# Turning two row groups of the first batch by DMA transposes, and loading batch 2's rows in quarters, in a spectral-filter and feed-forward kernel

## The chip, the cores and the metric

One Trainium2 chip, one of its cores. The metric is the device time of one launch in microseconds (us), the median of several runs. Runs of one kernel on one core agree to within some 0.3% here; the kernel before gave 776.29 to 777.75 us in the first three.

## The reference

For each of 8 batches of 3008 rows of 256 numbers, a real Fourier transform over the rows, a product with a complex filter and the inverse transform; the 24064 resulting rows then pass a feed-forward layer with 2048 inner features and a Swish with a slope of its own for each feature.

```python
X = np.fft.rfft(x, axis=1)
y = np.fft.irfft(X * (filt_r + 1j * filt_i)[None], n=x.shape[1], axis=1)
h = y.reshape(B * S, D) @ w_in
out = (h / (1.0 + np.exp(-beta * h))) @ w_out
```

## The kernel before

The transform is done with matmuls in stages: 3008 = 47 x 64. The feed-forward runs in 752 steps (47 blocks of 512 tokens, 16 feature groups each). A plan places the transform stages of the next batch between the steps: `place(a, z, units)` spreads units over steps a to z. The first batch comes ahead of step 0, for the most part. In its inverse stage, `z_t` holds the result, which must be turned (partitions and columns exchanged) before the last stage:

```python
z_t = ypool.tile([P, NDC, J, KP], BF16, ...)          # J = 32 rows, in 4 groups of JG = 8
...                                                   # in inverse3, for each pair of frequencies:
evac(z_t[:, :, :, 4*k0 : 4*k0+8]..., ps..., True)     # one ACT eviction of 512 columns
...
def turn_z(g, i, on_act=False):                       # row groups 1 to 3: two units each
    pz = fpsum.tile([P, 4, D], BF16, ...)
    for e in range(4):
        for dc in range(NDC):
            nc.tensor.transpose(pz[...], z_t[:, dc, JG*g + 4*i + e, :], ident[:])
    evac(zz0[g][:, 4*i : 4*i+4, :], pz[:KP], on_act)
```

A later batch b goes another way: its inverse stage writes z tiles, which SP's queue stores to a scratch tensor d in memory, and reads back turned. There are **two** buffers for z:

```python
zpool = pool("zpool", 2)
...
if kk == 0:
    s["z"] = zpool.tile([P, KG, D], BF16, name="z", tag="z")    # KG = 6 frequencies
...
evac(s["z"][:, kk : kk + 2, :], ps[:], True)                     # on ACT
if kk + 2 == KG:
    nc.sync.dma_start(s["d2c"][:, g*KG : (g+1)*KG, :], s["z"][:])
```

The output goes through `ost` tiles, stored from SP's queue. The last chunk's two half evictions (DVE and ACT) fill one tile, stored once.

## Time and profile before

| | before |
|---|---|
| time, median of the first 3 runs | 776.43 us |
| span of the profiled run | 775.3 us |
| PE busy | 767.5 us, 99% |
| ACT busy | 594.9 us, 77% |
| first feed-forward matmul | 37.02 us |
| granted clock | 1.0 |

PE is TensorE's matmuls, PEld its weight loads, DVE VectorE, ACT ScalarE, POOL GpSimd, SP the engine whose queue issues most transfers. PSUM is the memory that PE's matmuls write to; an eviction copies a tile out of it. `hps` is the first product of the feed-forward, `gT` its Swish, `acc` the second product. The granted clock is a share of PE's full clock. A line of a timeline gives the start, the duration, the engine and source line, and the instruction; in brackets, how long the engine had been idle and what ended that. The marks of blocks are the pieces of six "acc" matmuls in the chain of work that ended last.

### The profile page before, as it was taken

How to read it: one execution, taken by the hardware profiler on the slowest of the kernel's cores; microseconds unless marked ns; L12 is line 12 of the kernel's file. 1: busy time of each engine (PE TensorE's matmuls, PEld its weight loads, DVE VectorE, ACT ScalarE, POOL GpSimd, SP SyncE). 2: the span in 40 equal slices, each digit the busy share in tenths (PEclk: the TensorE clock that was granted, in tenths of full speed). 3: DMA queues.
4: the chain of work that ended last, by engine and by line, in shares of the span. 5: the costliest groups of instructions: out<-in, count | busy, mean ns of one | idle time of the engine just before them, and what ended most of it. 6: DMA issues, size and time to landing. Idle time of an engine off the chain costs nothing.

```text
span 775.3 us, 16219 instructions
## 1 busy us (share of the span) xinstructions
PE 767.5 (99%) x6444; PEld 554.2 (71%) x6444; DVE 379.3 (49%) x641; ACT 594.9 (77%) x926; POOL 142.8 (18%) x145
## 2 busy tenths in 40 slices
PE   8999999999999999999999999999999999999998
PEld 4877777777777777877768777787777776776665
DVE  7836846645446553474526735277353761401001
ACT  6888887886678867788677876778767787677776
POOL 7523401420013100231002410034000430000000
PEclk9999999999999999999999999999999999999999
DMA  7969755515911268022761237512451114100101
GB/s 170 240 164 191 169 164 106 136 55 155 177 43 68 89 145 161 30 85 85 160 134 47 78 116 146 106 64 80 130 110 55 49 69 129 56 28 28 55 28 55
DMA packets 103291, 80.48 MB, mean 104 GB/s; under 512 B 48466, under 2 KB 96996, under 8 KB 102258
## 3 DMA queue, kind: packets, MB, share of 16 engines
q1 hardware_dynamic: 100496, 63.73, 30.8%
q0 software_dynamic: 2720, 15.73, 10.5%
q8 instruction: 50, 0.82, 0.5%
q14 instruction: 25, 0.20, 0.1%
HBM read 46.15 MB, written 35.65 MB: 106 GB/s over the span
## 4 chain that ended last, share of the span: by engine, by line
PE 97%; ACT 1%; DMA 1%; POOL 0%; DVE 0%; issue 0%; POOLq 0%
PE acc L907 42%; PE hps L852 42%; PE ps L557 3%; PE ps L628 2%; PE ps L687 2%; PE ps L661 2%; DMA xg<-in_x_dram 1%; PE psz L477 1%; PE pz L549 0%; ACT a L109 0%; ACT a_t L109 0%; PE pb L403 0%; POOL xg L120 0%; PE ps L451 0%; PE ps2q L451 0%; PE pt L354 0%
## 5 line engine op out<-in xcount | busy, mean ns | idle before, releaser
L867 ACT ACTIVATE gT<-hps,beta_sb 128x512 bf16<-128x512 f32 x752 | 516.0, 688 | 166.8 <-PE hps L852 155.0
L907 PE MATMUL acc<-wout_sb,gT 128*128 128x256 bf16 x3008 | 451.6, 272 | 0.0
L852 PE MATMUL hps<-y,win_sb 128*128 128x512 bf16 (+8 forms) x1730 | 447.7, 351 | 0.0
L907 PEld LDWEIGHTS <-gT 128*128 128x128 bf16 x3008 | 279.6, 98 | 106.3 <-ACT gT L867 0.2
L852 PEld LDWEIGHTS <-win_sb 128*128 128x128 bf16 x1730 | 165.0, 98 | 24.4 <-issue 0.2
L677 POOL TENSOR_TENSOR v_t<-p_t,q_t 128x512 bf16<-128x512 f32 x84 | 106.7, 1270 | 383.9 <-DVE q_t L676 375.4
L111 DVE COPY ost<-acc 128x512 f32<-128x512 f32 (+2 forms) x89 | 56.6, 674 | 194.0 <-PE acc L907 188.4
L111 DVE CAST a<-ps 128x384 bf16<-128x384 f32 x96 | 53.5, 558 | 91.4 <-PE ps L628 91.2
L113 DVE TENSOR_SCALAR y<-ps 128x376 bf16<-128x376 f32 (+1 forms) x115 | 61.7, 544 | 59.5 <-PE ps L557 59.5
L672 DVE TENSOR_TENSOR p_t<-ps,frr 128x512 f32<-128x512 f32 x84 | 58.1, 692 | 33.5 <-PE ps L661 30.9
L676 DVE TENSOR_TENSOR q_t<-ps,fri 64x512 f32<-64x512 f32 x84 | 58.3, 694 | 1.2
L673 DVE SCALAR_TENSOR_TENSOR q_t<-ps,fri 64x512 f32<-64x512 f32 x84 | 57.4, 684 | 1.1
L557 PEld LDWEIGHTS <-zz 96*128 96x128 bf16 x512 | 35.3, 97 | 29.1 <-issue 0.3
L109 ACT ACTIVATE z<-ps 128x512 bf16<-128x512 f32 x84 | 49.6, 590 | 0.0
L628 PEld LDWEIGHTS <-xg 94*128 94x128 bf16 x448 | 30.7, 97 | 23.4 <-issue 0.4
L628 PE MATMUL ps<-t1b,xg 94*128 94x96 bf16 x448 | 36.7, 205 | 0.0
L557 PE MATMUL ps<-t,zz 96*128 96x94 bf16 x448 | 36.7, 204 | 0.0
L687 PE MATMUL ps<-v_t,t 128*128 128x256 bf16 x168 | 32.1, 273 | 0.0
L661 PE MATMUL ps<-a,t 128*128 128x256 bf16 x168 | 32.1, 273 | 0.0
L120 POOL DMA_DIRECT2D xg<-in_x_dram x22 | 12.1, 552 | 97.5 <-PE acc L907 93.9
L661 PEld LDWEIGHTS <-t 128*128 128x128 bf16 x168 | 15.7, 98 | 14.1
L687 PEld LDWEIGHTS <-t 128*128 128x128 bf16 x168 | 16.3, 98 | 6.4 <-DVE q_t L676 0.4
(118 smaller groups left out, 193.9 us busy)
## 6 DMA issues: line engine op xcount, KB each, us to landing
out_dram<-ost SPq DMA_DIRECT2D x80, 256.0 KB
d<-z SPq DMA_DIRECT2D x28, 384.0 KB
zz<-d SPq DMA_DIRECT2D x28, 384.0 KB
xg<-in_x_dram POOLq DMA_DIRECT2D x6, 1280.0 KB, 10.1
frr<-in_filt_r_dram SPq DMA_DIRECT2D x12, 256.0 KB
out_dram<-ost SPq DMA_DIRECT2D x20, 128.0 KB
frr<-in_moe_w_out_dram POOLq DMA_DIRECT2D x4, 512.0 KB, 12.8
xg<-in_x_dram POOLq DMA_DIRECT2D x6, 224.0 KB, 11.0
```

The source lines that it names most:

```text
L111: nc.vector.tensor_copy(dst, src)
L113: nc.vector.tensor_scalar_mul(dst, src, scale)
L557: nc.tensor.matmul(ps[:, e, :NP], lhsT=zz[:, jj + e, dc * P : (dc + 1) * P], rhs=tab[:], start=True, stop=True,)
L628: nc.tensor.matmul(ps[:, e, :KP], lhsT=s["x"][:, 4 * jq + e, dc * P : (dc + 1) * P], rhs=t1b[:], start=True, stop=True,)
L661: nc.tensor.matmul(ps[:, e, :], lhsT=t2[:, k0 + e, 3:5, :].rearrange("p c k -> p (c k)"), rhs=s["a2"][g][:, :, kk + e, :], start=True, sto ...
L672: nc.vector.tensor_tensor(p_t[:], ps[:], frr[:, ks_, :], ALU.mult)
L676: nc.vector.tensor_tensor(q_t[:M], ps[M:P], fri[M:P, ks_, :], ALU.mult)
L677: nc.gpsimd.tensor_tensor(v_t[:], p_t[:], q_t[:], ALU.add)
L687: nc.tensor.matmul(ps[:, e, :], lhsT=t3[:, k0 + e, :], rhs=v_t[:, e, :], start=True, stop=True)
L852: nc.tensor.matmul(hps[:, pos - t0 : pos - t0 + ln], lhsT=win_sb[:, dc, fb * P : (fb + 1) * P], rhs=ys[b][:, dc, n0 : n0 + ln], start=(dc ...
L867: nc.scalar.activation(gT[:, :tn], hps[:, :tn], ACT.Silu, scale=beta_sb[:, fb : fb + 1])
L907: nc.tensor.matmul(acc[tb // per][:, tb % per, :], lhsT=g_[:, tb * P : (tb + 1) * P], rhs=wout_sb[:, f_, :], start=(f_ == 0 and tb % per = ...
```

## The change

Its intent is to take matmul-engine transposes out of the stretch that PE limits, and to spread the load of batch 2's rows. Batch 1's own eight DMA transposes and the filter's loads, which stood together in SP's queue, are spread over steps there too. Cut to its core (the new layout of the zz tiles and the new order of batch 2's first stage are left out):

```diff
-    z_t = ypool.tile([P, NDC, J, KP], BF16, name="z_t", tag="y")
+    z_0 = a2pool.tile([P, NDC, JG, KP], BF16, name="z_0", tag="a2")
+    z_t = ypool.tile([P, NJG - 1, NDC, JG, P], BF16, name="z_t", tag="y")
+    gp.memset(z_t[:, :, :, :, KP:], 0.0)
...                                  # evictions: 128 columns to z_0 and 384 to z_t, was 512 to z_t
+    def read_z(g):
+        zz0[g] = zzpool.tile([P, NDC, JG, P], BF16, name="zz", tag="zz")
+        nc.sync.dma_start_transpose(zz0[g]..., z_t[:, g - 1]...)
...
-    place(15, 29, uz(2, True))       # with its two units of transposes
-    place(20, 24, units[:2], per=2)  # group 3's transposes
-    place(34, 58, units[2:])
+    place(23, 30, uz(2, True))
+    place(48, 59, uz(3))
...
-        place(at + 1, at + 1, [lambda: a2_read(1)] + uf(JG, NK), per=9)
+        place(at + 1, at + 1, [lambda: a2_read(1, (0,)), lambda: read_z(2)], per=9)
+        place(at + 2, at + 2, [lambda: a2_read(1, (1,))], per=9)
+        place(19, 19, uf(JG, 2 * JG) + [lambda: a2_read(1, (2,))], per=9)
+        place(21, 21, uf(2 * JG, NK) + [lambda: a2_read(1, (3,)), lambda: read_z(3)], per=9)
...
-        place(36, 36, ux(2), per=9)
-        at = place(52, 66, u1(2, True), per=3)
+        place(38, 50, ux(2, X_QUARTERS), per=9)
+        at = place(56, 69, u1(2, True), per=3)
...                                  # tail: each half its own tile and store, on SP and ACT
-                            evac(ost[:, c : c + per, cols], a[:, :, cols], half == 1)
+                            ost = pqpool.tile([P, 2, D], F32, name="ost", tag="pq"[half] + "_t")
+                            evac(ost[:, :1, :P], a[:, :, cols], half == 1)
+                            eng.dma_start(out[TOK - P :, cols], ost[:, 0, :P])
```

More of the change, by code (lines that the diff above doesn't have):

```diff
@@ L125 @@
     X_HALVES = [(0, 80, 0, J // 2), (80, NP, 0, J // 2), (0, 80, J // 2, J), (80, NP, J // 2, J)]
+    X_QUARTERS = [(p0, p1, g * JG, (g + 1) * JG) for g in range(NJG) for p0, p1 in ((0, 80), (80, NP))]
     X_FIRST = [(0, 80, 0, JG), (80, NP, 0, JG), (0, 80, JG, 2 * JG), (80, NP, JG, J)]
@@ L468, in inverse3 @@
         for j0, j1 in ((0, JG), (JG, J)) if last else ((0, J),):
-            nj = 4 * (j1 - j0)
+            ng = (j1 - j0) // JG
             if j0:
-                ps = fpsum.tile([P, 2, NDC, nj], F32, name="psz", tag="f")
+                ps = fpsum.tile([P, 2, ng, NDC, 4 * JG], F32, name="psz", tag="f")
             else:
-                ps = opsum.tile([P, 2, NDC, nj], F32, name="psz", tag="acc")
+                ps = opsum.tile([P, 2, ng, NDC, 4 * JG], F32, name="psz", tag="acc")
             for src, tab in ((p_t, t3), (q_t, t3b)):
@@ L477, in inverse3 @@
                         nc.tensor.matmul(
-                            ps[:, e, dc, :],
+                            ps[:, e, :, dc, :],
                             lhsT=src[:, e, dc * P : (dc + 1) * P],
-                            rhs=tab[:, k0 + e, 4 * j0 : 4 * j1],
+                            rhs=tab[:, k0 + e, 4 * j0 : 4 * j1].rearrange(
+                                "p (g r) -> p g r", g=ng
+                            ),
                             start=src is p_t and dc == 0 and e == 0,
@@ L484, in inverse3 @@
                         )
-            for e in range(2) if last else (None,):
-                if last:
-                    dst = z_t[:, :, j0:j1, 4 * (k0 + e) : 4 * (k0 + e) + 4]
-                    src = ps[:, e].rearrange("p c (j a) -> p c j a", a=4)
-                else:
-                    dst = z_t[:, :, :, 4 * k0 : 4 * k0 + 8].rearrange(
-                        "p c j (e a) -> p e (c j) a", e=2
-                    )
-                    src = ps.rearrange("p e c (j a) -> p e (c j) a", a=4)
-                evac(dst, src, not last or j0 > 0)
+            for e0, ne in ((0, 1), (1, 1)) if last else ((0, 2),):
+                cols = slice(4 * (k0 + e0), 4 * (k0 + e0 + ne))
+                if j0 == 0:
+                    evac(
+                        z_0[:, :, :, cols].rearrange("p c j (e a) -> p e (c j) a", a=4),
+                        ps[:, e0 : e0 + ne, 0].rearrange("p e c (j a) -> p e (c j) a", a=4),
+                        not last,
+                    )
+                if j1 == J:
+                    evac(
+                        z_t[:, :, :, :, cols].rearrange("p g c j (e a) -> p e (g c j) a", a=4),
+                        ps[:, e0 : e0 + ne, (JG - j0) // JG :].rearrange(
+                            "p e g c (j a) -> p e (g c j) a", a=4
+                        ),
+                        True,
+                    )
     def table4():
@@ L539 @@
     zz0[0] = apool.tile([P, NK * P], BF16, name="zz", tag="a1")
-    zz0[0] = zz0[0][:KP, : JG * D].rearrange("p (j d) -> p j d", j=JG)
+    zz0[0] = zz0[0][:, : JG * D].rearrange("p (c j d) -> p c j d", c=NDC, j=JG)
     def turn_z(g, i, on_act=False):
         if g not in zz0:
-            zz0[g] = zzpool.tile([KP, JG, D], BF16, name="zz", tag="zz")
-        pz = fpsum.tile([P, 4, D], BF16, name="pz", tag="f")
-        for e in range(4):
-            for dc in range(NDC):
-                nc.tensor.transpose(
-                    pz[:KP, e, dc * P : (dc + 1) * P], z_t[:, dc, JG * g + 4 * i + e, :], ident[:]
-                )
-        evac(zz0[g][:, 4 * i : 4 * i + 4, :], pz[:KP], on_act)
+            zz0[g] = zzpool.tile([P, NDC, JG, P], BF16, name="zz", tag="zz")
+        pz = fpsum.tile([P, NDC, 4, P], BF16, name="pz", tag="f")
+        for dc in range(NDC):
+            for e in range(4):
+                nc.tensor.transpose(pz[:KP, dc, e, :], z_t[:, g - 1, dc, 4 * i + e, :KP], ident[:])
+        evac(zz0[g][:KP, :, 4 * i : 4 * i + 4, :], pz[:KP], on_act)
+    def read_z(g):
+        zz0[g] = zzpool.tile([P, NDC, JG, P], BF16, name="zz", tag="zz")
+        nc.sync.dma_start_transpose(
+            zz0[g].rearrange("p c j d -> p (c j) d"),
+            z_t[:, g - 1].rearrange("p c j r -> p (c j r)"),
+        )
     def last4(zz, tab, jj, dc, dst, on_act, own=None, first=NP):
@@ L558, in last4 @@
                 ps[:, e, :NP],
-                lhsT=zz[:, jj + e, dc * P : (dc + 1) * P],
+                lhsT=zz[:KP, dc, jj + e, :],
                 rhs=tab[:],
@@ L586 @@
         if i % 2:
-            pz = opsum.tile([P, 2, D], BF16, name="pz", tag="acc")
+            pz = opsum.tile([P, NDC, 2, P], BF16, name="pz", tag="acc")
         else:
-            pz = fpsum.tile([P, 2, D], BF16, name="pz", tag="f")
+            pz = fpsum.tile([P, NDC, 2, P], BF16, name="pz", tag="f")
         for e in range(2):
             for dc in range(NDC):
-                nc.tensor.transpose(
-                    pz[:KP, e, dc * P : (dc + 1) * P], z_t[:, dc, 2 * i + e, :], ident[:]
-                )
-        evac(zz0[0][:, 2 * i : 2 * i + 2, :], pz[:KP], i % 2 == 1)
+                nc.tensor.transpose(pz[:KP, dc, e, :], z_0[:, dc, 2 * i + e, :], ident[:])
+        evac(zz0[0][:KP, :, 2 * i : 2 * i + 2, :], pz[:KP], i % 2 == 1)
     pw[0] = hpsum.tile([P, TB], F32, name="pw", tag="hps")
@@ L624, in s1 @@
         s = st[b]
-        jq, dc = divmod(i, NDC) if b == 1 else divmod(i, J // 4)[::-1]
+        jq, dc = divmod(i, NDC) if b < 3 else divmod(i, J // 4)[::-1]
         ps = fpsum.tile([P, 4, P], F32, name="ps1", tag="f")
@@ L640, in s1, with a2_read @@
         )
-    def a2_read(b):
+    def a2_read(b, gs=range(NG)):
         s = st[b]
-        s["a2"] = []
-        for g in range(NG):
+        for g in gs:
             t = a2pool.tile([P, NDC, KG, P], BF16, name="a2", tag="a2")
@@ L651, in a2_read @@
                 )
-            s["a2"].append(t)
+            s.setdefault("a2", []).append(t)
     def s23(b, i):
@@ L697, in zz_read @@
         for h in range(NJG):
-            t = zzpool.tile([KP, JG, D], BF16, name="zz", tag="zz")
-            nc.sync.dma_start(t[:], s["d2r"][:, h * JG : (h + 1) * JG, :])
+            t = zzpool.tile([P, NDC, JG, P], BF16, name="zz", tag="zz")
+            t = t[:KP].rearrange("p c j d -> p (c j d)").rearrange("p (j c d) -> p c j d", c=NDC, j=JG)
+            nc.sync.dma_start(
+                t.rearrange("p c j d -> p j c d"),
+                s["d2r"][:, h * JG : (h + 1) * JG, :].rearrange("r j (c d) -> r j c d", c=NDC),
+            )
             s["zz"].append(t)
@@ L746, in uz @@
     def uz(g, act=False):
-        return [lambda i=i: turn_z(g, i) for i in range(2)] + [
-            lambda i=i: last_z(g, i, act) for i in range(2 * NDC)
-        ]
+        return [lambda i=i: last_z(g, i, act) for i in range(2 * NDC)]
     def uf(a, z):
@@ L766, in ut, with ux, go @@
         ]
-    def ux(b):
-        def go():
-            xs[b] = load_x(b, X_WHOLE)
-        return [go]
+    def ux(b, parts=X_WHOLE):
+        def go(i):
+            xs[b] = load_x(b, parts[i : i + 2], xs.get(b))
+        return [lambda i=i: go(i) for i in range(0, len(parts), 2)]
     place(0, 0, rest, per=9)
-    place(1, 14, uz(1, True))
-    place(15, 29, uz(2, True))
-    units = uz(3, True)
-    place(20, 24, units[:2], per=2)
-    place(34, 58, units[2:])
+    place(1, 14, [lambda i=i: turn_z(1, i, True) for i in range(2)] + uz(1, True))
+    place(23, 30, uz(2, True))
+    place(48, 59, uz(3))
     first_step = [(S * b // TB) * NFB for b in range(B + 1)]
@@ L921 @@
                     if last and h == nch - 1:
-                        for half in range(2):
+                        for half, eng in ((0, nc.sync), (1, nc.scalar)):
                             cols = slice(half * P, (half + 1) * P)
-                            evac(ost[:, c : c + per, cols], a[:, :, cols], half == 1)
-                    else:
-                        evac(ost[:, c : c + per, :], a[:], on_act)
+                            ost = pqpool.tile([P, 2, D], F32, name="ost", tag="pq"[half] + "_t")
+                            evac(ost[:, :1, :P], a[:, :, cols], half == 1)
+                            eng.dma_start(out[TOK - P :, cols], ost[:, 0, :P])
+                        continue
+                    evac(ost[:, c : c + per, :], a[:], on_act)
                     store(t0 + h * per * P, per * P, ost[:, c : c + per, :])
```

## The prediction

> **What bounds the kernel now.** I read the page's busy table, then the chain of work that ended last, then the chain in order of time, and only then the stage that the change touches.
>
> ```profile
> PE 767.5 (99%) x6444; PEld 554.2 (71%) x6444; DVE 379.3 (49%) x641; ACT 594.9 (77%) x926; POOL 142.8 (18%) x145
> PE 97%; ACT 1%; DMA 1%; POOL 0%; DVE 0%; issue 0%; POOLq 0%
> ```
>
> The first line gives each engine's busy time; the second shares out the chain that ended last. PE (TensorE) is busy nearly throughout and is 97% of the chain. A busy PE need not be a full one, so I checked against the spacing of the matmuls. In the chain in order of time, a piece of six "acc" matmuls marks one 512-token block:
>
> ```profile
> 253.21 0.66 PE acc L907 x6
> ...
> 347.40 0.66 PE acc L907 x6
> ...
> 745.44 0.66 PE acc L907 x6
> ...
> 759.33 0.66 PE acc L907 x6
> ```
>
> At the end nothing but the feed-forward is left: a block takes 759.33 - 745.44 = 13.89 us, 0.868 us for each of 16 steps. In mid-kernel six blocks take 347.40 - 253.21 = 94.19 us. Six bare blocks are 83.3. Into these stretches go one batch's 48 matmuls of 256 columns, 0.109 us apart (5.2), and its 128 of 94 or 96 columns, about 0.0425 apart (5.4, from eight in 0.34 us in the timeline). The sum, 93.9, leaves 0.3. So PE has no holes worth the name once the blocks run, at about 37 us. Later work on DVE, ACT or the DMA queues is worth nothing unless it makes PE wait; PE work taken out is worth its full spacing. The rest is the start, 37 us, and the tail, some 3.5 us after the last matmul.
>
> The start needs its own reading. In its timeline from 22 us:
>
> ```profile
> 25.34 0.59 ACT L109 ACTIVATE z_t<-psz 128x512 bf16<-128x512 f32 x1
> 25.76 0.68 DVE L460 TENSOR_TENSOR pb_t<-ps,fri 128x512 bf16<-128x512 f32 x1
> 25.85 0.81 ACT L109 ACTIVATE a<-pb 128x768 bf16<-128x768 bf16 x1
> 26.36 0.68 DVE L460 TENSOR_TENSOR qb_t<-ps2q,fri 128x512 bf16<-128x512 f32 x1
> 26.64 0.60 ACT L109 ACTIVATE z_t<-psz 128x512 bf16<-128x512 f32 x1
> ```
>
> Columns: start, us, engine, line, instruction. DVE starts a product every 0.60 us, 1.20 us for a pair of frequencies, without a gap from 22.2 to 33.9. ACT has 0.51 + 0.71 = 1.22 us for the same pair. PE has 1.22. Three engines are balanced here, so anything added to ACT may show.
>
> **What the Trainium skill says.** "Perfetto Trace Analysis", section "Identifying the Most-Contended Engine", says that matmul busy share is a poor measure for PE, because matmuls are pipelined. The trace agrees: an acc matmul is listed with 272 ns and starts every 0.109 us. That is why I count spacings. "TensorE: Matmul & The Clock Gate", section "Part 4: PE-mode transpose", has a transpose as a matmul against an identity that lands in PSUM and needs a copy afterwards, with about 275 ns seen in one kernel. Here one is listed with 219 ns, but eight take 0.45 us, so it costs 0.056 us of PE. "DMA: Bandwidth & Descriptors", section "Latency and other measured facts", gives 261 GB/s for a DMA transpose with a non-contiguous middle dimension. Here eight of 128x768 in two-byte type (1.57 MB) took SP's queue 12.04 us, 131 GB/s: the measured rate is half, and I use it. Section "Issuing engines are not separate DMA queues" of the same page says that a second issuing engine saves only issue time; no run so far shows it for this kernel.
>
> **The change, part by part.**
>
> *Transposes removed from PE.* The 48 later transposes of batch 0 are six groups of eight. Four groups, those of row groups 2 and 3, go:
>
> ```profile
> L549 PE MATMUL pz<-ident,z_t 128*96 128x128 bf16 x48 | 3.7, 219 | 0.0
> 38.04 0.45 PE pz L549 x8
> 54.43 0.45 PE pz L549 x8
> 56.61 0.45 PE pz L549 x8
> ```
>
> 4 x 0.445 = 1.78 us, all of it in PE's full stretch: **-1.8 us**. Their four 0.69 us copies on DVE go too; DVE is not the bound there, so 0.
>
> *Evictions split at the start.* Of the inverse stage's twelve pairs, eleven had one ACT eviction of 512 columns; each becomes 128 to z_0 and 384 to z_t. The columns are the same. ACT's spacing of 0.51 us for 512 columns against 0.71 for 768 gives 0.2 us per 256, so 0.11 us fixed per instruction: an estimate of 11 x 0.11 = 1.2 us more ACT. About seven fall where ACT shares the bound (0.8 us), but ACT has short gaps there, about 0.9 us from 21 to 29 us, and three PSUM buffers between it and PE. In the later pairs ACT is idle 0.3 to 0.5 us each. I count **+0.3 us** (0 to 0.8). The last step's split was there before; the turning of row group 0 now waits for z_0 alone, worth under 0.1.
>
> *Memset of the padding.* 1536 elements on POOL. A POOL copy of 768 took 0.81 to 0.94 us, so an estimate of 1.5 us. POOL was idle 1.57 us at just that point, waiting for the filter. About 0, unless evictions to z_t are made to wait for it.
>
> *DMA transposes.* Two of 128x2048, 16 blocks of 128x128 each. At 12.04 / 48 = 0.25 us a block that is 4.0 us of queue each. Before, the queue of SP ran so:
>
> ```profile
> 52.97 12.04 SPq L648 DMA_TRANSPOSE a<-a  x8
> ...
> 69.07 10.42 SPq L826 DMA_DIRECT2D out_dram<-ost  x10
> ```
>
> Now it is: group 0 of batch 1 to about 56, z of row group 2 to about 60, landing 61 to 62; group 1 to 63; then block 0's stores, which before stood behind the eight filter loads; then filter quarter, group 2, filter quarter, group 3, z of row group 3, done near 80. The first consumer of row group 2 is at step 23. In the kernel before that step comes at about 62.9. Three removed groups (1.3) and three turned units of later place (0.5) bring it to about 61.1. So the data come within a microsecond of need: **+0.3 us** (0 to 1). Row group 3 is used from step 48, near 88 us: hidden. The filter's second quarter is needed by the fifth pair, at about 72, and would be issued at 67 to 69: also near, **+0.1**.
>
> *Batch 2's rows in quarters.* The same bytes in eight transfers, over steps 38 to 50. Before, they started at 81.7 us, and PE then worked 3.98 to 4.00 of every 4 us:
>
> ```profile
> 80.00:84.00 4.00, 3.98 (x33) 2.76 (x32) 3.88 (x7) 3.38 (x6) 3.47 (x4) 1.00 0.80 195
> 84.00:88.00 4.00, 4.00 (x31) 2.81 (x29) 2.67 (x4) 3.36 (x7) 1.40 (x2) 1.00 0.93 197
> ```
>
> Columns: window, its us, then busy of PE, PEld, DVE, ACT, POOL, granted clock, DMA share, GB/s. There was no PE wait to remove: **0**. Six more issues of 0.55 us on POOL are 3.3 us on an engine 18% busy.
>
> *Tail.* The last chunk's two half evictions ran one behind the other (DVE to 771.95, ACT from 771.98 to 772.26). They now have their own tiles and stores on two queues. At best ACT's 0.3 us vanish; the fixed part of a transfer stays. **-0.2 us**, provided the reads of the one PSUM bank are not themselves put in order.
>
> Sum: -1.8 + 0.3 + 0.3 + 0.1 - 0.2 = -1.3; 776.4 - 1.3 = **775.1 us**.
>
> **The rivals.** (a) *A DMA wait takes the place of the transposes.* For it: the 1 us margin at step 23 and a queue that works in order, behind transposes already irregular (0.25 us a block is a mean). Against it: DVE stood 2.37 us before an output eviction at 77.5 us in the kernel before, and PE lost 0.02 us, so DVE's waits are absorbed; but PE's own wait for its weights would not be. This would give 776.0 to 777.5. (b) *The start becomes longer*, because ACT takes over the bound, or because the first evictions wait for the memset. For it: the three balanced engines. Against it: ACT's gaps. It would give 775.5 to 776.5. (c) *All of it hides and the stores' earlier place pays too*: removal and tail in full, 774.3, or somewhat less. For it: block 0's stores free their buffers some 5 us sooner. Against it: PE did not wait for them, so there is nothing to win beyond the 1.8 and the tail.
>
> **Range and chances.** All three lie within 3 us of one another. From the full gain less a little luck, 773.9, to rival (a) with half a microsecond of start on top, 777.2. Two per cent is 15.5 us; no term is near it. Faster 0.005, same 0.985, slower 0.01: the last for a stall chain that I missed in the reordered queue.
>
> **What would show it.** Right: 16 instead of 48 matmuls in the pz group; the first hps matmul within 0.5 us of 37.0; blocks from the third on spaced as before; the mark of block 2, at 76.18 now, earlier by 1.3 to 1.8 us; eleven z_0 evictions of about 0.27 us on ACT. Wrong: an idle PE or PEld at the first ps matmul on row group 2 released by a DMA near 61 us (a); the first hps matmul at 37.6 or later with ACT waited for (b); the mark of block 3 moving otherwise than that of block 2, which would mean that batch 2's quarters or the filter cost or saved something. The prediction fails if PE idles over 2 us anywhere past 37 us, or if over 2 us vanish from the start.

## The result, and the profile after

The changed kernel takes **780.63 us** (779.42 to 781.42, 6 runs) against 776.32 (775.98 to 777.75, 6 runs). The ratio is 1.0052, with a 95% interval of 1.0039 to 1.0065. It is slower by half a per cent, clear of the noise though within the 2% that counts as the same, and outside the predicted range.

The page after, busy times and the shares of the chain that ended last:

```profile
PE 761.0 (98%) x6310; PEld 553.1 (71%) x6412; DVE 376.6 (48%) x639; ACT 595.9 (77%) x935; POOL 147.3 (19%) x152
PE 95%; ACT 2%; DVE 1%; issue 1%; DMA 1%; POOL 0%; ACTq 0%; DVEq 0%; POOLq 0%
```

PE is busy 6.5 us less, yet the span has grown from 775.3 to 777.7. The 6.5 us are no measure of the work removed: this trace has 6310 matmuls for 6412 weight loads, so some records are missing; e_third_tile below has 6412 of each and 764.7 us. The chain in order of time shows a hole. First two marks of the kernel before, then the kernel after:

```profile
76.18 0.66 PE acc L907 x6
...
92.77 0.66 PE acc L907 x6
```

```profile
36.15 1.02 PE hps L870 x6
...
73.27 0.66 PE acc L925 x6
...
82.79 7.89 DMA d<-z
90.77 0.32 ACT z L109
...
95.20 0.66 PE acc L925 x6
```

The block mark that stood at 76.18 is now at 73.27, the gain that was wanted and more (0.87 of the 2.91 us are an earlier start, by chance, as shown below). The next, at 92.77 before, is at 95.20. Between them the chain leaves PE for a store of z to the scratch tensor d. What ACT and PE did there (two timelines, ACT's lines first):

```profile
85.32 0.69 ACT L885 ACTIVATE gT<-hps,beta_sb 128x512 bf16<-128x512 f32 x1 [0.18 <-PE hps L870]
90.77 0.60 ACT L109 ACTIVATE z<-ps 128x512 bf16<-128x512 f32 x1 [4.76 <-DMA d<-z]
91.26 1.26 ACT L885 ACTIVATE gT<-hps,beta_sb 128x512 bf16<-128x512 f32 x2
```

```profile
87.40 0.60 PE L925 MATMUL acc<-wout_sb,gT 128*128 128x256 bf16 x4
91.99 1.01 PE L870 MATMUL hps<-y,win_sb 128*128 128x512 bf16 x2 [3.99 <-ACT gT L885]
92.80 0.63 PE L675 MATMUL ps<-a,t 128*128 128x256 bf16 x2
```

ACT stood 4.76 us before the first eviction into batch 1's **third** z tile, whose buffer is the first tile's and was still being stored. The Swish evictions (gT) that come behind it in ACT's program stood too; the next began only at 91.26. PE's next "hps" waits for one of them, with only two PSUM buffers for hps, so PE stood 3.99 us. The busy times by window (the window, its length, then PE, PEld, DVE, ACT, POOL, the granted clock, DMA share, GB/s) show what followed:

```profile
84.00:88.00 4.00, 4.00 (x32) 2.78 (x31) 2.98 (x5) 1.65 (x3) 2.52 (x5) 1.00 1.02 264
88.00:92.00 4.00, 0.01 (x2) 0.01 (x1) 0.82 (x2) 1.24 (x3) 1.07 (x1) 0.92 0.97 241
92.00:96.00 4.00, 4.00 (x21) 2.36 (x22) 2.42 (x4) 2.98 (x5) 0.21 (x1) 0.65 0.14 40
```

After the hole the clock is 0.65 on average: the pair of "hps" matmuls at 91.99 takes 0.81 us to the next instruction, where 0.43 is usual. The Trainium skill, "TensorE: Matmul & The Clock Gate", "Part 1: The HAM clock gate", says that PE falls to half its clock after an idle window of about 3.4 us and needs a busy one of like length to come back; this trace agrees on the fall: PE is idle from 88.00, and in finer windows the clock is 0.50 from about 91.4 to 94.7 us. It is back at 1.00 after some 2.7 us of work, sooner than the page's figure. Nothing of this was in the prediction's sum.

Why was the store late? SP's queue after:

```profile
71.51 3.01 SPq L662 DMA_TRANSPOSE a<-a  x2
74.56 4.22 SPq L566 DMA_TRANSPOSE zz<-z_t  x1
78.89 3.80 SPq L844 DMA_DIRECT2D out_dram<-ost  x5
82.79 1.10 SPq L706 DMA_DIRECT2D d<-z  x2
```

ACT had filled the first z tile at about 74.2 us (its third eviction starts at 73.62 and takes 0.62). The store was issued at 82.79, behind row group 3's transpose and five output stores, and landed at about 90.7. The tile was wanted near 86. Before, the store was issued at 79.58 and the third tile was not written until 89.16, with the whole program about 3 us later at that point:

```profile
79.58 7.49 SPq L692 DMA_DIRECT2D d<-z  x2
```

```profile
89.16 0.59 ACT L109 ACTIVATE z<-ps 128x512 bf16<-128x512 f32 x1
```

That was 9.6 us of room. The change moved the store 3.2 us later and the need 3.3 us earlier (85.90, from e_third_tile below); 3.1 us of room were left for a landing that took 7.9. Why the landing took so long was not tested. The DMA engines' share was 1.02 and 0.97 in the two windows from 84 to 92 us, so other transfers, batch 2's rows among them, probably slowed it; no run takes that load away with the store left late.

### The profile page after: what moved, and what is told of

It is laid out like the page before. It is cut to its first block, busy times and chain, and to the rows that moved or that the text cites. A ratio compares the mean times of both kernels' runs of the same rounds, so it can differ in the third digit from the quotient of the medians.

```text
span 777.7 us, 16072 instructions
## 1 busy us (share of the span) xinstructions
PE 761.0 (98%) x6310; PEld 553.1 (71%) x6412; DVE 376.6 (48%) x639; ACT 595.9 (77%) x935; POOL 147.3 (19%) x152
## 4 chain that ended last, share of the span: by engine, by line
PE 95%; ACT 2%; DVE 1%; issue 1%; DMA 1%; POOL 0%; ACTq 0%; DVEq 0%; POOLq 0%
PE acc L925 43%; PE hps L870 39%; PE ps L574 3%; PE ps L643 3%; PE ps L675 2%; PE ps L701 2%; DMA d<-z 1%; PE psz L481 1%; ACT a L109 0%; PE pb L404 0%; ACT a_t L109 0%; ACT gT L885 0%; ACT t L281 0%; ACT r L285 0%; PE ps L455 0%
## 5 line engine op out<-in xcount | busy, mean ns | idle before, releaser
L870 PE MATMUL hps<-y,win_sb 128*128 128x512 bf16 (+8 forms) x1630 | 426.9, 350 | 4.0 <-ACT gT L885 4.0
L113 DVE TENSOR_SCALAR y<-ps 128x376 bf16<-128x376 f32 (+1 forms) x119 | 63.9, 545 | 60.9 <-PE ps L574 60.8
L120 POOL DMA_DIRECT2D xg<-in_x_dram x28 | 15.3, 550 | 97.7 <-PE acc L925 93.9
## 6 DMA issues: line engine op xcount, KB each, us to landing
xg<-in_x_dram POOLq DMA_DIRECT2D x5, 1280.0 KB, 10.1
```

The lines of the kernel that those rows point to most:

```text
L113: nc.vector.tensor_scalar_mul(dst, src, scale)
L870: nc.tensor.matmul(hps[:, pos - t0 : pos - t0 + ln], lhsT=win_sb[:, dc, fb * P : (fb + 1) * P], rhs=ys[b][:, dc, n0 : n0 + ln], start=(dc ...
```

## The experiments

**Theory Q** (queue): the loss is that one stall, caused by the place of the store in SP's in-order queue, plus the clock's fall after it; the rest of the change gains about 2 us. **Rival C** (contention): the quarters of batch 2's rows disturb other transfers and work at many places. All results were correct.

### e_third_tile: one more buffer, no transfer moved

The z pool keeps its two buffers; the third tile comes from the a2 pool, which has tiles of the same size, one of them free at this time.

```diff
-                s["z"] = zpool.tile([P, KG, D], BF16, name="z", tag="z")
+                if b == 1 and g == 2:
+                    s["z"] = a2pool.tile([P, KG, D], BF16, name="z", tag="a2")
+                else:
+                    s["z"] = zpool.tile([P, KG, D], BF16, name="z", tag="z")
```

> The changed kernel with one buffer more: batch 1's third z tile comes from the a2 pool (free there), so its eviction on ACT need not wait for the store of the first z tile. No transfer is added, removed or moved. Theory Q (queue): the loss is one stall near 88 us, ACT held at that tile until the late store of d lands, and PE's 4 us of idleness is followed by a halved clock for some us; everything else of the change gains. Then no PE wait over 0.5 us past 37 us, the granted clock is 1.0 throughout and the time is 773.5 to 775.5. Rival C (contention: the quarters of batch 2's rows slow other work broadly, in several places): at least 2 us of the loss remains, 778 or more.

774.28 us (773.93 to 774.67, 4 runs), ratio to the kernel before 0.9970 (0.9953 to 0.9986). The SP queue and ACT's evictions in this run:

```profile
82.76 1.10 SPq L709 DMA_DIRECT2D d<-z  x2
```

```profile
82.86 0.59 ACT L109 ACTIVATE z<-ps 128x512 bf16<-128x512 f32 x1
85.90 0.59 ACT L109 ACTIVATE z<-ps 128x512 bf16<-128x512 f32 x1
```

```profile
89.68 0.66 PE acc L928 x6
```

The store is as late as in the changed kernel, and nobody waits for it. The block mark of 73.27 is the same to the hundredth in both; the next is at 89.68 here and at 95.20 there. Of these 5.52 us, 3.99 are PE's hole; the other 1.53 fit the slow clock (4 us at 0.65 lose 1.4). The medians lie 6.35 us apart. The profiled run of the changed kernel was the fastest of its six, with a mean clock of 0.998; the three slowest have 0.996, so the slow stretch was probably longer in them, but they have no trace.

### e_rows_whole: batch 2's rows in one go again

```diff
-        place(38, 50, ux(2, X_QUARTERS), per=9)
+        place(36, 36, ux(2), per=9)
```

> The changed kernel with batch 2's rows loaded whole at step 36 again, all else as changed. Theory Q: the store of d is still issued only at about 82 to 83 us, behind the z transpose and the output stores, so ACT still waits for it, 2 to 6 us; time 778 to 782. Rival C: the stall is the quarters' doing, the store lands in time and the time is 773.5 to 775.5.

782.85 us (781.97 to 783.41), ratio 1.0077 (1.0062 to 1.0092): worse still, and a little above the range that theory Q gave.

```profile
93.82 0.60 ACT L109 ACTIVATE z<-ps 128x512 bf16<-128x512 f32 x1 [7.03 <-DMA d<-z]
```

The store, issued at 83.62, took 10.1 us to land behind the whole batch, and PE stood 6.3 us. So the quarters are not the harm: in the presence of the late store they save about 2 us (782.85 against 780.63, in different rounds). Rival C falls here, and in e_third_tile, where the quarters are in place and no loss is left.

### b_quarters: the quarters alone, on the kernel before

```diff
-        place(36, 36, ux(2), per=9)
-        at = place(52, 66, u1(2, True), per=3)
+        place(38, 50, ux(2, X_QUARTERS), per=9)
+        at = place(56, 69, u1(2, True), per=3)
```

> The kernel before with only the quarters of batch 2's rows (and the later steps and order of its first stage that go with them). PE waited for nothing in that stretch, so both the prediction and theory Q expect no change: 775.8 to 777.0. The rival, that quarters are a gain or a loss by themselves, expects 1 us or more either way.

776.15 us (775.86 to 776.73) against 776.17, ratio 0.9997 (0.9984 to 1.0010). Alone they are worth nothing, as predicted.

### e_group3_on_pe: one DMA transpose less in the queue

```diff
-        place(21, 21, uf(2 * JG, NK) + [lambda: a2_read(1, (3,)), lambda: read_z(3)], per=9)
+        place(21, 21, uf(2 * JG, NK) + [lambda: a2_read(1, (3,))], per=9)
+        place(20, 24, [lambda i=i: turn_z(3, i) for i in range(2)], per=9)
```

> The changed kernel with row group 3 turned on PE again (16 transposes at steps 20 and 24), so that one 128x2048 DMA transpose less stands in SP's queue ahead of the output stores and of d. Theory Q: the store of d is issued about 4 us sooner (near 78.5 us), ACT does not wait for it, PE has 0.9 us more work; time 774.5 to 776.5. Rival C: the quarters still meet the store of d and most of the stall remains, 778 or more.

775.15 us (774.90 to 775.60), ratio 0.9980 (0.9965 to 0.9995). The store is issued at 79.50, ACT does not wait, and 16 transposes back on PE cost 0.87 us against e_third_tile, near the 16 x 0.056 = 0.90 of the estimate (the four-run medians are not sharp enough to say more).

### e_early_turns: the same transposes, issued while the queue is idle

```diff
+        place(9, 9, [lambda: read_z(2)], per=9)
+        place(11, 11, [lambda: read_z(3)], per=9)
-        place(at + 1, at + 1, [lambda: a2_read(1, (0,)), lambda: read_z(2)], per=9)
+        place(at + 1, at + 1, [lambda: a2_read(1, (0,))], per=9)
```

(with `read_z(3)` taken from step 21)

> The changed kernel with both DMA transposes issued early: row group 2 at step 9, row group 3 at step 11, where SP's queue is otherwise idle from 47 to 52 us; the rest of its order is kept. Theory Q: the store of d is issued about 4 us sooner, no stall at 88 us, PE keeps the whole 1.8 us; time 773.5 to 775.0. Group 0 of batch 1 comes 4 us later than before, and may make PE wait up to 1 us at step 20. Rival C: 778 or more.

774.26 us (774.18 to 774.38), ratio 0.9968 (0.9953 to 0.9983). Its SP queue:

```profile
47.94 5.00 SPq L566 DMA_TRANSPOSE zz<-z_t  x1
...
73.72 3.75 SPq L846 DMA_DIRECT2D out_dram<-ost  x5
77.56 0.54 SPq L706 DMA_DIRECT2D d<-z  x1
```

The store is issued 5.2 us sooner than in the changed kernel. No PE wait at step 20 either. Its four runs are the closest together of all.

### e_store_on_act: only the store moves, to another queue

```diff
-                nc.sync.dma_start(s["d2c"]...)
+                (nc.scalar if b == 1 and g == 0 else nc.sync).dma_start(s["d2c"]...)
```

> The changed kernel, but batch 1's first store of d is issued from ACT's queue, right after ACT's own eviction, so it need not stand behind the z transpose and five output stores in SP's queue. It tells the place in the queue from the load of the DMA engines. If the place in SP's queue is all: issued near 80.4 instead of 82.8 us, landing some 2.4 us sooner, ACT's wait falls from 4.8 to about 2.4 us, PE's idleness to under 2 us[...]; 775.5 to 777.0. If the landing is set by the transfers already under way (8 us from issue to landing in the profile of the changed kernel): the stall stays nearly whole, 779 to 781.

773.92 us (773.81 to 774.07), ratio 0.9967 (0.9954 to 0.9980). I had expected the issue near 80.4 us; it was

```profile
74.18 0.35 ACTq L706 DMA_DIRECT2D d<-z  x1
```

because the tile is full by then: in SP's queue the store had stood ready for 8.6 us. The whole stall goes with its place in the queue, though every transfer is still made, and the time is below both ranges that I had given. Taken again as e_store_on_act2:

> The run with batch 1's first store of d on ACT's queue, taken again, to stand beside the next one on the same chip: 773.8 to 774.4, and no PE wait past 37 us.

774.37 us (774.10 to 775.82), ratio 0.9977 (0.9964 to 0.9991). The profiled run of it has one PE wait past 37 us, of 0.5 us, for row group 2's transpose, which was issued at 55.97 and landed near 61.95, so the expectation of no such wait was missed: the narrow margin at step 23 that the prediction feared is real, but it shows only in some runs.

### e_tail_old: what the new tail is worth

The run with the third tile, with the old tail put back (both halves into one `ost` tile, one store).

> The run with the third z tile from the a2 pool, but with the old tail: both half evictions into one tile and one store. In the profiles ACT still begins its half only after DVE's, in the new tail as in the old, and from PE's last matmul to the end it is 3.6 against 3.7 us. So 774.4, 0.0 to 0.2 us over that run; the prediction had 0.2, with 0.3 as the most.

774.00 us (773.92 to 774.50), ratio 0.9970 (0.9958 to 0.9982), the same ratio as with the new tail. The new tail in e_third_tile:

```profile
768.71 0.29 DVE L111 COPY ost<-acc 128x128 f32<-128x128 f32 x1 [0.40 <-PE acc L928]
769.04 0.28 ACT L109 ACTIVATE ost<-acc 128x128 f32<-128x128 f32 x1 [1.21 <-DVE ost L111]
```

ACT still waits for DVE, though the two write different tiles now. Both still read the same PSUM tile (`acc`), which is the likely reason; no run tests it. So there was nothing to gain from the evictions.

### All row groups by DMA: four tries at a better kernel

*e_all_groups_dma* turned row group 1 by a DMA transpose as well (`read_z(1)` at step 2, its last-stage units at steps 11 to 14), on top of the early turns.

> The run with early turns, with row group 1 too turned by a DMA transpose, at step 2, and its four last-stage units at steps 11 to 14: no transposes are left on PE but those of row group 0. PE loses 16 more, 0.9 us. If the data are in time (SP's queue is held by an earlier wait until about 44 us, landing near 48, first needed near 49): 773.2 to 773.7. If the transposes now crowd batch 1's first group out, PE waits at step 20 and the time is 774 or more.

777.74 us (776.74 to 780.03), ratio 1.0018 (1.0003 to 1.0033): a loss. PE's two long waits in it name both causes (engine, line, what it waited for, us in total, times, longest):

```profile
PE ps L574 <- DMA zz<-z_t: 2.1, 1, 2.1
PE ps L675 <- DMA a<-a: 2.0, 1, 2.0
```

After both the granted clock stayed at 1.00: these holes were half as long as that of the changed kernel.

*e_all_groups_later* keeps the changed kernel's order for the other two, with the store of d on ACT's queue, and moves the four units to steps 13 and 14.

> The same with row group 1 turned by a DMA transpose too, issued first in SP's queue after its wait at 44 us, with nothing of the kind behind it until batch 1's group 0; its four last-stage units at steps 13 and 14 instead of 1 to 14. In the failed run with all groups the data of row group 1 were there at 50.1 us, with two transposes queued; here they should be there sooner and are wanted near 50. Expected: 16 transposes less on PE, 0.9 us, so 773.0 to 773.4; if PE waits for these data or at the change to block 1, 773.9 or more.

775.55 us (775.38 to 777.40), ratio 0.9994 (0.9982 to 1.0007), above the expected 773.0 to 773.4. The two waits are gone, and PE begins its last run of 20 matmuls at 765.87 us, where e_store_on_act begins it at 766.05; but the span ends at 773.7 against 772.1. The tail of this run:

```profile
769.03 0.41 SPq L945 DMA_DIRECT2D out_dram<-ost  x1
769.12 2.44 ACTq L945 DMA_DIRECT2D out_dram<-ost  x1
```

The issue of the last store on ACT's queue took 2.44 us; it is 0.37 to 0.38 in the other profiles of the new tail that show it. Two more runs put the last store elsewhere: *e_all_groups_old_tail* with the old tail, and *e_all_groups_tail_on_sp* with two tiles and two stores, both from SP.

> All groups by DMA with row group 1's units at steps 13 and 14, but with the old tail (one store on SP's queue for both halves). In the profile of the run before, PE reached block 47 0.2 us sooner than without, but the last store's issue on ACT's queue took 2.44 us in place of 0.38. If that issue is what cost it: 773.2 to 773.8. If the loss is elsewhere (the waits at the first blocks), 775 or more stays.

> The same with the new tail's two tiles and two stores kept, both issued from SP. If the long issue belongs to ACT's queue: 773.3 to 773.9, at most 0.4 us over the old tail, for the one issue of 0.41 us more in a row. If it belongs to having two stores of half the columns: 775 or more.

774.10 us (773.36 to 774.91), ratio 0.9973 (0.9960 to 0.9986), and 774.60 us (773.97 to 777.53), ratio 0.9987 (0.9976 to 0.9999). In both profiles the long issue is gone, and with it 1.2 to 1.9 us of the tail; the times point the same way, but both intervals overlap that of e_all_groups_later, that of the old tail narrowly. The first lies a little above its expected 773.2 to 773.8, the second above its range as well. From the start of the last 20 matmuls to the end of the span it is 5.95 us with the old tail, 6.65 with both on SP, 7.83 with the long issue, 6.06 in the changed kernel and 6.17 in the kernel before. Only one run of each build has a trace, and why that issue was long I cannot say.

The all-groups kernel does not beat e_early_turns. Its 16 transposes fewer should be worth 0.9 us; in the profile of e_all_groups_later PE waits 0.3 us for ACT in the first steps, and from the first psz piece to the last run of matmuls it gains 0.41 us on e_store_on_act. I did not trace the rest.

## Why the prediction was wrong

*The step that failed* is in "DMA transposes": "Row group 3 is used from step 48, near 88 us: hidden." The data were indeed in time for their own consumer. But a transfer in an in-order queue delays all that is issued behind it, and I followed only the stores of the output. I listed the queue until row group 3 was "done near 80", which was close (78.8), and did not ask what came next. What came next was the store of d, on which ACT's third z tile waits, with only two buffers. The sum has no term for this wait; it measured 5.52 us in the profile. The prediction's own sign came true, "PE idles over 2 us anywhere past 37 us", and its chance of 0.01 was set aside for "a stall chain that I missed in the reordered queue"; it named the kind of event and did not follow it to a buffer. Rival (a) had the right kind of event, a DMA wait in place of the transposes, at the wrong place (61 us in place of 88) and through the wrong engine. Its argument that "DVE's waits are absorbed" was then no reason for comfort about ACT, which carries every Swish eviction; and the PE hole also cost clock: 3.99 us became 5.52.

*The rate of the queue* was misread as well. Its "the measured rate is half" takes the time that SP's queue was held for the time of the transfers. The 4.0 us expected for each 128x2048 transpose came out as 1.60 and 4.22 in the changed kernel, and in e_store_on_act2 one held the queue for 1.59 us and landed 6.0 us after its issue. That the queue came to "near 80" all the same was partly luck: 1.60 + 4.22 us are 2.2 under the 8.0 expected.

*Transposes removed from PE*, -1.8: right. From b_quarters, whose start is equal, to e_third_tile, the mark of block 3 moves from 91.76 to 89.68 and that of block 4 from 109.68 to 107.82, 1.86 us.

*Evictions split at the start*, +0.3: in fact 0. From the first psz piece to the first hps piece of the chain it is 16.24 us before (20.78 to 37.02) and 16.24 after (19.91 to 36.15). ACT did pay, in the groups by line:

```profile
L109 ACT ACTIVATE z_t<-psz 128x384 bf16<-128x384 f32 x11 | 5.5, 503 | 0.0
L109 ACT ACTIVATE z<-psz 128x128 bf16<-128x128 f32 x11 | 3.1, 286 | 1.1 <-PE psz L481 1.1
```

503 + 286 against 594 ns is 0.195 us of busy time more for a pair, above the estimate of 0.11, but nothing of it reached the chain. The 0.87 us by which the profiled start is earlier after comes ahead of that stage, where the first kernel's trace waited for the rows of x until 10.4 us; e_store_on_act2 starts at 36.97 and e_store_on_act, the same program, at 36.08, so it is chance. For this reason the sign "the first hps matmul within 0.5 us of 37.0" could not tell.

*Memset*, about 0: right; it took 1.37 us on POOL against the 1.5 estimated.

*Row group 2 at step 23*, +0.3: 0 in most profiles, 0.5 in one. *The filter's second quarter*, +0.1: no PE wait for it in the changed kernel's trace. *Quarters*, 0: right alone, but they softened the stall by about 2 us. *Tail*, -0.2: about 0, as the prediction's proviso allowed: the two evictions are still in order. Without the stall the sum of what was measured is about -1.9, against -1.3 predicted; e_third_tile measured 774.28 against the 775.1 predicted, and the number of rival (c), 774.3, fits it. Its reason, that the stores' earlier place pays, is not shown: the transposes removed are worth 1.9 us by themselves.

## What to carry to other kernels

When a transfer is added to an in-order queue, follow the queue past it, to every transfer behind it, and ask for each which buffer it frees, who needs that buffer when, and how many buffers there are. A saving that makes the consumer earlier eats the same room as the queue that gets longer. Where PE is the bound and ACT carries its evictions, a long wait of ACT becomes a wait of PE (here 4.76 us became 3.99), and that hole cost clock as well; issuing the added transfers early, in the queue's idle time, kept the whole gain (776.5 to 774.3 us).

## What the Trainium skill lacked or had wrong

- "DMA: Bandwidth & Descriptors", section "Issuing engines are not separate DMA queues", says that issuing from several engines saves only the issue time, "which is usually small relative to the DMA itself". The section lacks the time that a ready transfer stands behind others in one queue: one store moved from SP's queue to ACT's was issued at 74.18 in place of 82.79 us, and the kernel went from 780.63 to 773.92 us.
- The same page has no figure for an issue that takes long now and then: the last store's issue on ACT's queue took 2.44 us in one profile, 0.37 to 0.38 in others. The cause is open.
- The same page, "Latency and other measured facts", gives 261 GB/s for a DMA transpose with a non-contiguous middle dimension, but not how long one holds the queue that issues it: eight transposes of 196 KB held SP's queue for 12.04 us, and a 128x2048 one held it for 1.46 to 6.32 us in these runs. These are not transfer times, so they do not show the page's rate wrong.
